# Low-plane scores by 64-row matmuls: both heads side by side, tiles two by two, one PSUM bank per head

## The chip, the core and the metric

The kernel runs on one core of one Trainium2 chip. The core has a matmul engine (TensorE, in the profile PE for matmuls and PEld for weight loads), VectorE (DVE), ScalarE (ACT), GpSimd (POOL) and SyncE (SP, which here only issues DMAs). Matmuls write to PSUM, which has eight banks of 2 KB per partition; everything else lives in SBUF, 128 partitions wide. The metric is the device time of one execution in microseconds, lower is better.

## The reference

Eight batches, eight heads of 64 dimensions, 512 local and 32 global positions. Local queries see all global keys and the local keys at most 32 positions away; global queries see everything. A feed-forward part with a cosine gate follows.

```python
s_g = scale * q_g @ concat(k_g, k_l).T ;  out_g = softmax(s_g) @ concat(v_g, v_l)
s_ll = where(|pos_q - pos_k| <= 32, scale * q_l @ k_l.T, -1e9)
out_l = softmax(concat(scale * q_l @ k_g.T, s_ll)) @ concat(v_g, v_l)
x = concat(out_g, out_l)  as (8*544, 512)
h = x @ w_in  (512 -> 2048);  out = (h * cos(h)) @ w_out  (2048 -> 512)
```

All inputs and the output are f32. The sums need more digits than one f16 matmul gives, so the kernel splits operands into a high and a low f16 plane.

## The kernel before

**Slots.** The whole work is written out by hand as events in numbered slots (`at(slot, phase, f, ...)`, line 1181). Inside a slot events are emitted in the order of their phase. A slot of the steady part holds one step of the feed-forward part (`m1_a` to `m1_d`, `m2_a`: 24 matmuls of 256 columns and 12 of 512, then elementwise work on ACT, DVE and POOL) and a few attention steps. Sixteen slots pass per batch, four per pair of heads. `steady` (line 1216) gives each step of a pair its slot. From the emitted order, a planner with a timeline of its own makes the final order of each engine: an instruction with no bank or operand ready in that timeline is passed by others. On the chip each engine's order is then fixed.

**Batches 0 and 1** take another path (`attn_pair_f`): scores straight from f32, 64 rows each, two heads in two banks (`f_qk`, line 607). It stays as it is.

**Batches 2 to 7**, one pair of heads at a time (24 pairs): `load_qk` brings queries (64 partitions) and keys (the other 64) of both heads; `qk_a` to `qk_c` find a scale, through a small matmul `pm_qk` (line 478) into PSUM; `qk_d` (lines 536, 537) writes the high plane to `qa` and the low plane to `kl`, each [128, 2 heads, 608]. `qk_e` (line 542) then moves partitions by DMAs from SP, in three steps that follow one another:

- step 0: high keys `qa[64:128]` to both halves of `kh` (lines 546, 547)
- step 1: low queries `kl[0:64]` to `qa[64:128]` (line 549)
- step 2: low keys `kl[64:128]` to `kl[0:64]` (line 551)

So `qa` holds high over low queries, `kh` the high keys twice and `kl` the low keys twice. `sc_a` (line 788) makes the scores of one tile of 128 queries against its window of 192 or 224 keys. Each head has two 128-row matmuls, with `kh` (line 794) and with `kl` (line 795), so that all four products of planes are summed. Both heads' scores go to one bank, `ps`. `sc_b` (line 810) reads them with VectorE, adds the mask and finds the row minimum `mn` (line 811); `sc_c` takes the exponential on ScalarE (line 440 is the helper `table_act`), `sc_d` normalises and splits, `sc_e` transposes by DMA, `av_a` multiplies with the values (`acc`, line 938). Pairs with an odd number also carry the global scores of two pairs, `g_a` (line 968), in two pieces: four heads in four column strips of 32, each with `kh` and then `kl` (line 977).

**Slots of the pieces before.** Counted from a pair's own slot t: copies at t-9 (steps 0 and 1) and t-8 (step 2), tiles 0 to 3 at t-7, t-6, t-5, t-4, each scored and read in its slot, the exponentials at t-4, global pieces at t-7 and t-6, the values at t. The next pair's `pm_qk` falls into slot t-7.

**PSUM.** Of the eight banks three have the tag "ph" (feed-forward in), two "po" (feed-forward out) and three "att". The scores `ps`, the global scores `gps`, `pm_qk` and `pm_v`, `acc` and `gacc` (the global output, line 1034) all take turns in the three of "att"; each is free again when its reader on VectorE (or ScalarE) is through.

Of the kernel before, what the change touches and what calls it, by code (L numbers as in the profile page):

```python
# [10 lines left out]
F32 = mybir.dt.float32  # L11
# [8 lines left out]
P = 128  # L20
# [3 lines left out]
SG = 32  # L24
# [12 lines left out]
WIN = ((0, 192), (128, 224), (256, 224), (416, 192))  # L37
OFF = (0, 0, 0, 32)
QZ = (32, 160, 320, 448)
WINF = ((0, 192), (128, 224), (256, 224), (384, 224))  # L40
MOFF = (0, 192, 416, 672)
MOFF_F = (0, 192, 416, 640)
# [48 lines left out]
s_load = -13  # L91
s_qa = -12
s_qd = -10
s_qe0 = -9
s_qe1 = -9
s_qe2 = -8
# [45 lines left out]
def body(tc, qk, qkf, v, wi, wo, mask, out):  # L142
    nc = tc.nc
# [4 lines left out]
    with ExitStack() as ctx:  # L148
        cp = ctx.enter_context(tc.tile_pool(name="cp", bufs=1))
        ap_ = ctx.enter_context(tc.tile_pool(name="ap", bufs=2))  # L150
        ps = ctx.enter_context(tc.tile_pool(name="ps", bufs=3, space=PSUM))
# [8 lines left out]
        msk = cp.tile([P, MW], BF16, name="msk")  # L160
# [3 lines left out]
        for i in range(4):  # L164
            t = cp.tile([P, 2, 2, 256], F16, name=f"planes{i}")
# [268 lines left out]
        st = {}  # L434
# [107 lines left out]
        def qk_e(b, p, k):  # L542
            qa, kh, kl, _ = st["qk", b, p]
            move = nc.vector.tensor_copy if b == 0 and SHV[p] else nc.sync.dma_start
            if k == 0:
                move(kh[0:64], qa[64:128])
                move(kh[64:128], qa[64:128])
            elif k == 1:
                move(qa[64:128], kl[0:64])
            else:  # L550
                move(kl[0:64], kl[64:128])

        def v_a(b):
            m = ap_.tile([P, 1], F32, tag="vm", name=f"vm_{b}")
# [52 lines left out]
        def f_qk(b, p, hf):  # L607
# [4 lines left out]
            for i in (2 * hf, 2 * hf + 1):  # L612
                z, w = WINF[i]
                for h in range(2):
                    r = slice(64 * h, 64 * h + 64)
                    nc.tensor.matmul(
                        pt[h][:, i % 2, :w], q[r, QZ[i] : QZ[i] + P], k[r, z : z + w],
                        start=True, stop=True,
# [3 lines left out]
        def f_tt(b, p, hf):  # L622
# [3 lines left out]
            for i in (2 * hf, 2 * hf + 1):  # L626
                w = WINF[i][1]
                t = ap_.tile([P, 2, w], F32, tag="t", name=f"t_{b}_{p}_{i}", bufs=6)
# [32 lines left out]
        def f_tr(b, p, hf):  # L661
# [4 lines left out]
            for k in range(2):  # L666
                tr = ps.tile([P, 4, P], F32, tag="att" if b else "ph", name=f"ftr_{b}_{p}_{hf}_{k}")
                n = 96 if k else P
                for i in range(2):
                    w = WINF[2 * hf + i][1] - P if k else P  # L670
                    for h in range(2):
# [12 lines left out]
        def f_av(b, p, hf):  # L684
# [9 lines left out]
            for n, (i, k, tl, q0, w) in enumerate((  # L694
                (i0, 0, i0, 0, 128), (i0 + 1, 0, i0 + 1, 0, 128 if hf == 0 else 96),
                (i0, 1, i0 + 1, 64 if hf == 0 else 32, 64 if hf == 0 else 96), (i0 + 1, 1, i0 + 2, 0, 128),
            )):
                kn = WINF[i][1] - P if k else P
                for h in range(2):
# [86 lines left out]
            )  # L786

        def sc_a(b, p, i):
            qa, kh, kl, al = st["qk", b, p]
            z, w = WIN[i]  # L790
            pt = ps.tile([P, 2, w], F32, tag="att", name=f"ps_{b}_{p}_{i}")
            for h in range(2):
                q = qa[:, h, QZ[i] : QZ[i] + P]
                nc.tensor.matmul(pt[:, h], q, kh[:, h, z : z + w], start=True, stop=False)
                nc.tensor.matmul(pt[:, h], q, kl[:, h, z : z + w], start=False, stop=True)
            st["ps", b, p, i] = pt

        def sc_b(b, p, i):
            w = WIN[i][1]
            al = st["qk", b, p][3]  # L800
            pt = st.pop(("ps", b, p, i))
            if b > 1 and i >= 2:
                if i == 2:
                    st["raw", b, p] = w2.tile([P, 512], I64, tag="raw", name=f"t_{b}_{p}_2")
                rf = st["raw", b, p].bitcast(F32)
                t = rf[:, (i - 2) * 512 : (i - 2) * 512 + 2 * w].rearrange("p (a b) -> p a b", a=2)
            else:
                t = ap_.tile([P, 2, w], F32, tag="t", name=f"t_{b}_{p}_{i}", bufs=6)
            mn = ap_.tile([P, 2], F32, tag="mn", name=f"mn_{b}_{p}_{i}", bufs=8)
            for h in range(2):  # L810
                nc.vector.tensor_tensor_reduce(  # L811
                    t[:, h], pt[:, h], msk[:, MOFF[i] : MOFF[i] + w], al, 3.0e38,
                    ALU.add, ALU.min, mn[:, h : h + 1],
                )
            if b < 2 and DEFN[b]:
                nc.vector.tensor_scalar(mn, mn, 14 * math.log(2.0), None, op0=ALU.add)
            st["t", b, p, i] = (t, mn)
# [150 lines left out]
        def g_a(b, g, k):  # L968
            z, w = GW[k]
            pt = ps.tile([P, w], F32, tag="att", name=f"gps_{b}_{g}_{k}")  # L970
            for hh in range(4):
                qa, kh, kl, _ = st["qk", b, 2 * g + hh // 2]
                h = hh % 2
                o = pt[32 * hh : 32 * hh + 32]
                q = qa[:, h, 0:SG]
                for kk in (kh, kl):
                    nc.tensor.matmul(
                        o, q, kk[:, h, z : z + w], start=(kk is kh), stop=(kk is kl),
                        tile_position=(0, 32 * hh), skip_group_check=True,
                    )  # L980
            st["gps", b, g] = pt

        def g_b(b, g, k):
# [197 lines left out]
        def at(slot, phase, f, *a):  # L1181
            ev[slot].append((phase, len(ev[slot]), f, a))

        def attn_pair(b, p, o):
            at(o["load"], PJ, load_qk, b, p)
            at(o["qa"], PF, qk_a, b, p)
            if o["tight"] or QB == 0:
                at(o["qa"], PG, qk_b, b, p)
                at(o["qa"], PG2, qk_c, b, p)
            else:  # L1190
                at(o["qa"] + 1, PA, qk_b, b, p)
                at(o["qa"] + 1, PB, qk_c, b, p)
            at(o["qd"], PF2, qk_d, b, p)
            for k in range(3):
                at(o["qe"][k], PA0 if k == 0 or o["tight"] else PJ, qk_e, b, p, k)
            for i in range(4):
                at(o["sc"][i], PA, sc_a, b, p, i)
                at(o["sc"][i], PA if o["tight"] else PC, sc_b, b, p, i)
                at(o["ex"], PI, sc_c, b, p, i)
                at(o["sd"], PF, sc_d, b, p, i)  # L1200
                at(o["tr"][i], PA2, sc_e, b, p, i)
            at(o["vd"], PF2, v_d, b, p)
            at(o["av"], PA, av_a, b, p)
            at(o["av"] if b else -6, PF, av_b, b, p)
            if p % 2:
                g = p // 2
                for k in range(2):
                    at(o["gs"][k], PA, g_a, b, g, k)
                    at(o["gs"][k], PA if o["tight"] else PC, g_b, b, g, k)
                at(o["ex"], PI, g_c, b, g)  # L1210
                at(o["gd"], PF2, g_d, b, g)
                at(o["ge"], PA2, g_e, b, g)
                at(o["gf"], PG, g_f, b, g)
                at(o["gf"], PH2, g_g, b, g)

        def steady(t, late=False):
            o = dict(
                load=t + s_load, qa=t + s_qa, qd=t + s_qd, qe=(t + s_qe0, t + s_qe1, t + s_qe2),
                sc=[t + s_sc0, t + s_sc1, t + s_sc2, t + s_sc3], ex=t + s_ex, sd=t + s_sd,
                tr=(t + s_tr,) * 4, vd=t + s_vd, av=t + s_av, gs=(t + s_gs0, t + s_gs1),  # L1220
                gd=t + s_gd, ge=t + s_ge, gf=t + s_gf, tight=False,
            )
            if late:
                o |= dict(load=t - 11, qa=t - 10, qd=t - 9, qe=(t - 8,) * 3)
            return o

        def tight(u, vd):
# [68 lines left out]
        for b in range(2, B):  # L1296
            t = 16 * (b - 1) + T0[b > 2]
            tv = max(t + s_v, 9)
            at(tv, PA0, load_v, b)
            at(tv + 1, PF, v_a, b)  # L1300
            at(tv + (1 if b == 2 else 2), PG if b == 2 else PA, v_b, b)
            at(tv + (1 if b == 2 else 2), PG2 if b == 2 else PB, v_c, b)
            for p in range(NPAIR):
                attn_pair(b, p, steady(t + 4 * p, b == 2 and p == 0))
# [52 lines left out]
def _mask():  # L1357
# [3 lines left out]
    cols = []  # L1361
    for i, (z, w) in enumerate(WINF):
        q = np.arange(i * P, (i + 1) * P)[:, None]
# [43 lines left out]
```

## Time and profile before

| | |
|---|---|
| median of 3 runs | 1025.35 us (1020.35 to 1028.5) |
| profiled execution | 1024.95 us, span 1022.9 us |
| granted TensorE clock, mean | 0.949 |
| PE busy | 917.1 us, 90% of the span |
| DVE, ACT, POOL busy | 644.6, 643.2, 621.7 us |
| 0 to 215 us, PE busy | 159.13 us (clock 0.79) |
| 215 to 845 us, PE busy | 589.36 of 630 us (clock 0.99) |
| 845 to 1022.9 us, PE busy | 168.57 of 177.9 us |

The first stretch is the start: weights, batches 0 and 1. The second holds the attention of batches 2 to 7 beside the feed-forward part. In the last one only the feed-forward part is left. A matmul's duration in the trace includes its way through the array, so that durations overlap; the distance from one start to the next tells what it costs. A line number such as L795 is that of the kernel before. A note in brackets at the end of a timeline row is the idle time before it and what ended it.

### The profile page before, as it was taken

How to read it: one execution, taken by the hardware profiler on the slowest of the kernel's cores; microseconds unless marked ns; L12 is line 12 of the kernel's file. 1: busy time of each engine (PE TensorE's matmuls, PEld its weight loads, DVE VectorE, ACT ScalarE, POOL GpSimd, SP SyncE). 2: the span in 40 equal slices, each digit the busy share in tenths (PEclk: the TensorE clock that was granted, in tenths of full speed). 3: DMA queues.
4: the chain of work that ended last, by engine and by line, in shares of the span. 5: the costliest groups of instructions: out<-in, count | busy, mean ns of one | idle time of the engine just before them, and what ended most of it. 6: DMA issues, size and time to landing. Idle time of an engine off the chain costs nothing.

```text
span 1022.9 us, 20754 instructions
## 1 busy us (share of the span) xinstructions
PE 917.1 (90%) x7847; PEld 626.1 (61%) x7847; DVE 644.6 (63%) x1575; ACT 643.2 (63%) x1298; POOL 621.7 (61%) x817
## 2 busy tenths in 40 slices
PE   7755788899888998998899899999999999999996
PEld 5534455566565666665676566666666666666662
DVE  5986867477767776767585758676866643332330
ACT  6543787657677576776677667767776775444330
POOL 4491564646675876775767476757676778444440
PEclk7756698999999999999999999999999999999999
DMA  9438013034545764453536454555454423000000
GB/s 376 170 122 347 1 42 108 1 122 125 122 90 120 137 141 104 103 120 117 122 84 130 127 124 93 124 142 124 92 118 98 100 43 76 1 22 1 22 21 21
DMA packets 141147, 106.11 MB, mean 104 GB/s; under 512 B 120440, under 2 KB 120440, under 8 KB 139000
## 3 DMA queue, kind: packets, MB, share of 16 engines
q1 hardware_dynamic: 141048, 104.80, 39.9%
q8 instruction: 61, 1.00, 0.4%
q14 instruction: 38, 0.31, 0.1%
HBM read 51.82 MB, written 8.91 MB: 59 GB/s over the span
## 4 chain that ended last, share of the span: by engine, by line
PE 30%; POOL 20%; DVE 19%; DMA 12%; ACT 11%; issue 6%; SPq 1%; POOLq 0%; ACTq 0%; DVEq 0%
PE ph L1096 13%; POOL t L873 6%; POOL planes L883 6%; DMA qkr<-qk 6%; PE po L1154 4%; PE po L1152 4%; PE po L1153 4%; ACT t L440 4%; DVE kl L537 3%; POOL w L1131 3%; DMA vr<-v 2%; DVE qm L496 2%; DVE u L1119 2%; ACT L440 2%; DVE gf L1133 2%
## 5 line engine op out<-in xcount | busy, mean ns | idle before, releaser
L1096 PE MATMUL ph<-xh,wi_h 128*128 128x256 f16 x1024 | 283.1, 277 | 17.4 <-DVE gf L1133 11.6
L1096 PE MATMUL ph<-xl,wi_h 128*128 128x256 f16 x1024 | 282.5, 276 | 0.9 <-DVE xl L718 0.9
L1096 PE MATMUL ph<-xh,wi_l 128*128 128x256 f16 x1024 | 282.3, 276 | 0.0
L1096 PEld LDWEIGHTS <-wi_h 128*128 128x128 f16 x2176 | 212.4, 99 | 69.3 <-issue 35.0
L1138 POOL TENSOR_TENSOR gl<-gf,gh 128x512 f16<-128x512 f32 x136 | 160.3, 1179 | 140.6 <-ACT gh L1137 140.6
L1152 PE MATMUL po<-wo_h,gh 128*128 128x512 f16 x544 | 206.9, 380 | 7.9 <-DVE o L1160 7.8
L1153 PE MATMUL po<-wo_l,gh 128*128 128x512 f16 x544 | 206.8, 380 | 0.0
L1154 PE MATMUL po<-wo_h,gl 128*128 128x512 f16 x544 | 206.6, 381 | 0.1
L1131 POOL TENSOR_TENSOR w<-w 128x512 f32<-128x512 f32 x136 | 145.6, 1071 | 77.8 <-ACT w L440 77.4
L1119 DVE SCALAR_TENSOR_TENSOR u<-u,cm,ph 128x512 f32<-128x512 f32 x136 | 101.2, 744 | 121.6 <-ACT u L1118 121.4
L1133 DVE SCALAR_TENSOR_TENSOR gf<-w,ph 128x512 f32<-128x512 f32 x136 | 93.1, 685 | 121.7 <-POOL w L1131 121.5
L1137 ACT CAST gh<-gf 128x512 f16<-128x512 f32 x136 | 83.3, 612 | 128.8 <-DVE gf L1133 127.4
L440 ACT ACTIVATE t<-t,mn 128x224 f32<-128x224 f32 (+1 forms) x256 | 117.3, 459 | 58.0 <-DVE mn L811 45.9
L873 POOL TENSOR_TENSOR t<-t,sm 128x192 f32<-128x192 f32 (+1 forms) x192 | 100.9, 557 | 78.2 <-DVE sm L858 76.1
L440 ACT ACTIVATE w<-u,ca 128x512 f32<-128x512 f32 x136 | 97.8, 721 | 74.8 <-DVE u L1119 71.5
L883 POOL TENSOR_TENSOR planes<-t,planes 128x192 f16<-128x192 f32 (+1 forms) x192 | 118.4, 646 | 0.0
L1096 PEld LDWEIGHTS <-wi_l 128*128 128x128 f16 x1088 | 107.4, 99 | 16.2 <-issue 2.2
L1118 ACT ACTIVATE u<-ph,cm 128x512 f32<-128x512 f32 x136 | 92.0, 677 | 14.1 <-PE ph L1096 14.0
L1154 PEld LDWEIGHTS <-gl 128*128 128x128 f16 x544 | 53.2, 98 | 62.9 <-issue 0.6
L1153 PEld LDWEIGHTS <-gh 128*128 128x128 f16 x544 | 53.2, 98 | 59.0 <-issue 10.7
L1152 PEld LDWEIGHTS <-gh 128*128 128x128 f16 x544 | 53.2, 98 | 49.3 <-issue 0.9
L440 ACT ACT_TABLE_LOAD x59 | 75.7, 1283 | 2.7 <-DVE gmn L744 1.7
(203 smaller groups left out, 1411.7 us busy)
## 6 DMA issues: line engine op xcount, KB each, us to landing
qkr<-qk SPq DMA_DIRECT2D x24, 608.0 KB, 4.7
vr<-v SPq DMA_DIRECT2D x8, 1280.0 KB, 8.6
out<-o SPq DMA_DIRECT2D x34, 256.0 KB, 2.0
kh<-qa SPq DMA_DIRECT2D x48, 152.0 KB, 2.6
wo_h<-wo SPq DMA_DIRECT2D x8, 512.0 KB, 4.4
wo_l<-wo SPq DMA_DIRECT2D x8, 512.0 KB, 4.8
raw_wo<-wo SPq DMA_DIRECT2D x8, 512.0 KB, 3.6
qa<-kl SPq DMA_DIRECT2D x24, 152.0 KB, 2.5
```

What stands on the lines that cost most here:

```text
L440: ins = nc.scalar.activation(*a, **k).ins
L873: nc.gpsimd.tensor_tensor(t[:, h], t[:, h], rb[:, h], op=ALU.mult)
L883: nc.gpsimd.tensor_tensor(lo[:, h], t[:, h], hi[:, h], op=ALU.subtract)
L1096: nc.tensor.matmul(ph[:, a], w[:, kc, f], x[:, kc, q], start=first and ip == 0, stop=last and ip == 2, skip_group_check=True,)
L1118: nc.scalar.activation(u, ph, AF.Identity, bias=m)
L1119: nc.vector.scalar_tensor_tensor(u, u, m, ph, op0=ALU.subtract, op1=ALU.subtract)
L1131: nc.gpsimd.tensor_tensor(w, w, w, op=ALU.mult)
L1133: nc.vector.scalar_tensor_tensor(gf, w, 0.5, st.pop(("ph", c, j)).rearrange("p a b -> p (a b)"), op0=ALU.subtract, op1=ALU.mult,)
L1138: nc.gpsimd.tensor_tensor(gl, gf, gh, op=ALU.subtract)
L1152: nc.tensor.matmul(po[k], gh[:, q], wo_h[:, f], start=(f == 0), stop=False)
L1153: nc.tensor.matmul(po[k], gh[:, q], wo_l[:, f], start=False, stop=False)
L1154: nc.tensor.matmul(po[k], gl[:, q], wo_h[:, f], start=False, stop=(f == NJ - 1))
```

## The change

For batches 2 to 7, the product of low queries with low keys is dropped, and the low keys meet the high queries alone, with 64 rows.

- The copies have four steps. Step 2 moves only head 0's low keys to the lower half. Step 3, new, moves head 1's high queries to the upper half of `kl`'s first slot, which step 2 has read. Head 0 then finds high queries and low keys on partitions 0 to 63, head 1 on 64 to 127. Steps 2 and 3 are both in slot t-8.
- `sc_a` works on tiles 0 and 1 at t-7 and on 2 and 3 at t-5, and does nothing at t-6 and t-4. It takes two banks, one for each head, and both tiles of a head share one (224 columns each). First come the four 128-row matmuls with `kh`, then four of 64 rows, the heads in turn. The reads by `sc_b` stay in their slots; each reads from both banks.
- `g_a` makes the four matmuls with `kh` first and then four 64-row ones.

```diff
-            else:
-                move(kl[0:64], kl[64:128])
+            elif k == 2:
+                move(kl[0:64, 0], kl[64:128, 0])
+            else:
+                move(kl[64:128, 0], qa[0:64, 1])
...
         def sc_a(b, p, i):
+            if i % 2:
+                return
             qa, kh, kl, al = st["qk", b, p]
-            z, w = WIN[i]
-            pt = ps.tile([P, 2, w], F32, tag="att", name=f"ps_{b}_{p}_{i}")
-            for h in range(2):
-                q = qa[:, h, QZ[i] : QZ[i] + P]
-                nc.tensor.matmul(pt[:, h], q, kh[:, h, z : z + w], start=True, stop=False)
-                nc.tensor.matmul(pt[:, h], q, kl[:, h, z : z + w], start=False, stop=True)
-            st["ps", b, p, i] = pt
+            pt = [
+                ps.tile([P, 2, FW], F32, tag="att", name=f"ps_{b}_{p}_{i // 2}_{h}") for h in range(2)
+            ]
+            for ii in range(i, i + 2):
+                z, w = WIN[ii]
+                for h in range(2):
+                    nc.tensor.matmul(
+                        pt[h][:, ii % 2, :w], qa[:, h, QZ[ii] : QZ[ii] + P], kh[:, h, z : z + w],
+                        start=(ii == i), stop=False, skip_group_check=True,
+                    )
+            for ii in range(i, i + 2):
+                z, w = WIN[ii]
+                for h in range(2):
+                    r = slice(64 * h, 64 * h + 64)
+                    nc.tensor.matmul(
+                        pt[h][:, ii % 2, :w], (kl if h else qa)[r, 0, QZ[ii] : QZ[ii] + P],
+                        kl[r, h, z : z + w], start=False, stop=(ii > i), skip_group_check=True,
+                    )
+                st["ps", b, p, ii] = [pt[h][:, ii % 2, :w] for h in range(2)]
...
-                for kk in (kh, kl):
-                    nc.tensor.matmul(
-                        o, q, kk[:, h, z : z + w], start=(kk is kh), stop=(kk is kl),
-                        tile_position=(0, 32 * hh), skip_group_check=True,
-                    )
+                nc.tensor.matmul(
+                    o, q, kh[:, h, z : z + w], start=True, stop=False,
+                    tile_position=(0, 32 * hh), skip_group_check=True,
+                )
+            for hh in range(4):
+                qa, kh, kl, _ = st["qk", b, 2 * g + hh // 2]
+                h = hh % 2
+                r = slice(64 * h, 64 * h + 64)
+                nc.tensor.matmul(
+                    pt[32 * hh : 32 * hh + 32], (kl if h else qa)[r, 0, 0:SG], kl[r, h, z : z + w],
+                    start=False, stop=True, skip_group_check=True,
+                )
...
-            for k in range(3):
+            for k in range(4):
                 at(o["qe"][k], PA0 if k == 0 or o["tight"] else PJ, qk_e, b, p, k)
```

More of the change, by code (lines that the diff above doesn't have):

```diff
@@ L39 @@
 QZ = (32, 160, 320, 448)
+FW = 224
 WINF = ((0, 192), (128, 224), (256, 224), (384, 224))
@@ L811, in sc_b @@
                 nc.vector.tensor_tensor_reduce(
-                    t[:, h], pt[:, h], msk[:, MOFF[i] : MOFF[i] + w], al, 3.0e38,
+                    t[:, h], pt[h], msk[:, MOFF[i] : MOFF[i] + w], al, 3.0e38,
                     ALU.add, ALU.min, mn[:, h : h + 1],
@@ L1217, in steady @@
             o = dict(
-                load=t + s_load, qa=t + s_qa, qd=t + s_qd, qe=(t + s_qe0, t + s_qe1, t + s_qe2),
+                load=t + s_load, qa=t + s_qa, qd=t + s_qd, qe=(t + s_qe0, t + s_qe1, t + s_qe2, t + s_qe2),
                 sc=[t + s_sc0, t + s_sc1, t + s_sc2, t + s_sc3], ex=t + s_ex, sd=t + s_sd,
@@ L1223, in steady @@
             if late:
-                o |= dict(load=t - 11, qa=t - 10, qd=t - 9, qe=(t - 8,) * 3)
+                o |= dict(load=t - 11, qa=t - 10, qd=t - 9, qe=(t - 8,) * 4)
             return o
```

## The prediction

> **What bounds the kernel now.** I read the page first, then the busy time by stretch, then the waits of the matmul engine, then the timelines of PE, DVE and SP in one stretch of the steady part.
>
> ```profile
> span 1022.9 us, 20754 instructions
> ...
> PE 917.1 (90%) x7847; PEld 626.1 (61%) x7847; DVE 644.6 (63%) x1575; ACT 643.2 (63%) x1298; POOL 621.7 (61%) x817
> ...
> PE   7755788899888998998899899999999999999996
> ...
> PEclk7756698999999999999999999999999999999999
> ```
>
> ```profile
> 215.00:845.00 630.00, 589.36 (x5484) 406.51 (x5482) 441.43 (x1062) 442.67 (x913) 431.30 (x572) 0.99 0.49 111
> ```
>
> The second fence is the stretch in which batches 2 to 7 go through the changed code (columns: length, then busy time of PE, PEld, DVE, ACT, POOL, then granted clock, DMA share, GB/s). PE is busy 589.36 of 630.00 us at a clock of 0.99; the next busiest engine has 442.67. So PE's order of work sets the end, and time goes in or out in two ways: array time per matmul, and holes in PE's stream. The holes of the whole run, by who ended them:
>
> ```profile
> PE ph L1096 <- DVE gf L1133: 11.6, 17, 1.8
> PE pm_qk L478 <- DVE mn L811: 10.0, 4, 2.8
> PE po L1152 <- DVE o L1160: 7.8, 7, 2.0
> PE ps L795 <- DMA kl<-kl: 3.5, 3, 2.4
> PE gacc L1034 <- DVE mn L811: 3.1, 4, 0.9
> ```
>
> (Total us, times, longest.) The second and the fifth are waits for a PSUM bank: pm_qk and gacc take a bank of the tag "att" and stand until VectorE has read a score tile (mn, line 811) out of it. The fourth is the wait for the key-plane copy that this change lengthens.
>
> **Array time of the scores.** One tile pair of the steady part, on PE:
>
> ```profile
> 501.00 0.25 PE L794 MATMUL ps<-kh,qa 128*128 128x192 f16 x1
> ...
> 501.25 0.25 PE L795 MATMUL ps<-kl,qa 128*128 128x192 f16 x1
> 501.43 0.32 PE L977 MATMUL gps<-kh,qa 128*32 128x288 f16 x4
> 501.56 0.31 PE L977 MATMUL gps<-kl,qa 128*32 128x288 f16 x4
> 501.80 0.23 PE L478 MATMUL pm_qk<-d_qk,ones 128*128 128x128 bf16 x1
> ...
> 507.07 0.26 PE L794 MATMUL ps<-kh,qa 128*128 128x224 f16 x1
> ...
> 507.36 0.26 PE L795 MATMUL ps<-kl,qa 128*128 128x224 f16 x1
> 507.55 0.30 PE L977 MATMUL gps<-kh,qa 128*32 128x256 f16 x4
> ```
>
> Durations overlap, so what counts is start to start. Four 192-column matmuls start at 501.00 to 501.25, so 0.083 us each; four of 224 from 507.07 to 507.36, so 0.097. A pair of heads has four low-plane tiles for two heads: 2 x (0.083 + 0.097 + 0.097 + 0.083) = 0.72 us. If the 64-row matmuls of the two heads run at once, 0.36 of that goes, in 24 pairs 8.6 us. Whether they do is shown by the 64-row f32 scores of batch 0, two stretches right behind one another:
>
> ```profile
> 19.59 1.76 PE L616 MATMUL fps<-kf,qf 64*128 64x192 f32 x8
> ```
>
> ```profile
> 21.14 1.70 PE L616 MATMUL fps<-kf,qf 64*128 64x224 f32 x4
> ```
>
> The four records of 21.14 are, as I read their even steps, one head alone: 1.70 less the last one's tail, 0.58, over three steps is 0.373 per 224 columns, 0.320 per 192. The eight of 19.59 are both heads, four of each width: one after the other they would take 2.77 us and the tail's rest of 0.2; they took 1.76. So two heads side by side do run in about half, in f32. For f16 I take the same.
>
> The number of matmuls and of weight loads stays (16 and 16 per pair). What is added is changes of the array's shape. The same rows price one: from 501.25 a 192-column matmul should be followed at 501.33, and the first 32-column tile starts at 501.43, so 0.10; from 507.36 + 0.097 to 507.55 it is 0.09. Back again: the four 288-column low matmuls start together at 501.56, 288 columns take 0.125 at this rate, and pm_qk starts at 501.80, 0.10 after that and the starts' 0.02. Into the 64-row shape, from full-array matmuls 0.109 apart:
>
> ```profile
> 133.79 0.27 PE L1096 MATMUL ph<-xl,wi_h 128*128 128x256 f16 x1
> 133.90 0.27 PE L1096 MATMUL ph<-xh,wi_l 128*128 128x256 f16 x1
> 134.10 1.02 PE L616 MATMUL fps<-kf,qf 64*128 64x224 f32 x4
> ```
>
> 134.10 less 133.90 is 0.20, so again 0.09. I take 0.10 for each, in and out. An even pair gets two low blocks, each between full-array work: four changes, 0.40 us against 0.36 saved. An odd pair has the global scores too. At the slot of its tile 0 the order was full, 32 columns, full (two changes) and becomes full, 64 rows, 32 columns, 64 rows by 32 columns, full (four); at tile 1's slot the scores are gone and the global block has one change more; tiles 2 and 3 add two: five, 0.50 us. So 12 x (0.40 + 0.50) = 10.8 us against 8.6: **+2.2 us**. The Trainium skill, page "TensorEngine Tiling (Array Packing)", section Theoretical Speedup, promises up to 2x when the contracted dimension is 64 or less; by that alone this term would be -8.6, and its list of key properties adds that a change of mode drains the array, which the 0.09 to 0.10 us here agree with.
>
> The global low plane stays as long as it was, since its four tiles ran side by side already, and 64-row by 32-column tiles do too: here the four first ones start within 0.02 us.
>
> ```profile
> 162.53 0.43 PE L731 MATMUL fgps<-qkr 64*32 64x288 f32 x2
> 162.54 0.43 PE L731 MATMUL fgps<-kf,qf 64*32 64x288 f32 x2
> 162.79 0.41 PE L731 MATMUL fgps<-qkr 64*32 64x288 f32 x2
> ```
>
> **The copies on SP.** The third move halves in bytes and a fourth follows that overwrites what the third reads, so SP waits for its landing. Pair 12:
>
> ```profile
> 517.71 0.46 SPq L549 DMA_DIRECT2D qa<-kl  x1
> 518.23 0.58 SPq L455 DMA_DIRECT2D qkr<-qk  x1
> 520.03 0.46 SPq L551 DMA_DIRECT2D kl<-kl  x1
> 534.56 0.46 SPq L546 DMA_DIRECT2D kh<-qa  x1
> ```
>
> ```profile
> 527.67 0.25 PE L794 MATMUL ps<-kh,qa 128*128 128x192 f16 x1
> ```
>
> ```profile
> DMA to landing us min/median/max: 2.3/3.2/7.8
> ```
>
> (The last is line 551's copy.) Move to move is 520.03 - 517.71 = 2.3 us. The fourth would go out near 522.4 and land near 525, against 527.67: hidden, with 2 to 3 us left of 5. Behind it on SP stand transposes, output stores and the next pair's first copy; here SP has nothing to issue until 534.56, and 24 issues of 0.46 us are 11 us of a queue that is mostly idle. Where the third copy is late (up to 7.8 us, and PE already waits three times, 3.5 us) the fourth adds its 2.3 to 3.2. Ends: 0, and 12.5 (five such pairs at 2.5, more than the three that are late now). I take the low side, **+2**, since the typical pair has room.
>
> **The PSUM banks.** Tag "att" has three. Two tiles by two heads are still four tiles in a pair, but they are taken two at once and each is held until both of its tiles are read. VectorE reads late:
>
> ```profile
> 505.50 0.41 DVE L811 CUSTOM_DVE_ANT_0 t<-ps,msk,al 128x192 f32<-128x192 f32 x1
> 505.83 0.08 DVE L811 DVE_READ_ACCUMULATOR2_ANT mn<- 128x1 f32 x1
> 505.83 0.41 DVE L811 CUSTOM_DVE_ANT_0 t<-ps,msk,al 128x192 f32<-128x192 f32 x1
> ...
> 506.17 0.51 DVE L994 CUSTOM_DVE_ANT_0 gt<-gps,zero,gal 128x288 f32<-128x288 f32 x1
> ...
> 506.61 0.28 DVE L510 TENSOR_REDUCE r<-pm_qk 128x2 f32<-128x128 f32 x1
> ```
>
> The tile written at 501.00 is read from 505.50 on. In an odd pair tile 0 (501.00), the global scores (501.43) and pm_qk (501.80) fill the three banks now. Afterwards the two score tiles and the global scores do, and pm_qk of the next pair waits until about 506.7. The planner will set it later in PE's order; what it misjudges becomes a hole. Rows for such a hole:
>
> ```profile
> 511.48 0.24 PE L1034 MATMUL gacc<-ptg,vh 128*64 128x32 f16 x4 [0.74 <-DVE mn L811]
> ```
>
> ```profile
> 581.95 0.27 PE L478 MATMUL pm_qk<-d_qk,ones 128*128 128x128 bf16 x1 [2.84 <-DVE mn L811]
> ```
>
> 0.74 is a matmul that the planner had placed where it thought the bank was free, which is the case here, so I take that: 12 odd pairs x 0.74 = 8.9 us, less the 3.1 of gacc, whose slot no longer has a score tile: **+5.8** (ends -3.1 and 12 x 2.84 = 34). The Trainium skill, same page, Gotcha 1: PSUM Pressure, says that row tiles write to different banks and so press on PSUM: it speaks against the change here, and no figure of it is used.
>
> **What comes earlier.** Tiles 1 and 3 are scored a slot before their turn, so VectorE can read them as soon as it is free, and ScalarE's exponentials wait for those reads now:
>
> ```profile
> L440 ACT ACTIVATE t<-t,mn 128x224 f32<-128x224 f32 (+1 forms) x256 | 117.3, 459 | 58.0 <-DVE mn L811 45.9
> ```
>
> An exponential that starts earlier lets ScalarE reach the next chunk's work earlier, and with it the reads that PE waits for (gf 11.6, o 7.8, together 19.4). Ends 0 and -19.4; ScalarE is idle for 45.9 us there but is no bound, so I take a fifth: **-4**.
>
> Sum on the profiled execution, 1024.95 us (span 1022.9 and 2.05 around it): +2.2 +2 +5.8 -4 = +6.0, 1031. The median of the runs, 1025.35, is 0.4 above it, which changes nothing: **1031 us**, 0.6% over.
>
> **Rivals.** *Banks bind* (slower): the hole at pm_qk is not 0.74 but 1.5 us, between the two rows, because VectorE reads the tile only after the next chunk's work; and the early reads give nothing back. 12 x 1.5 - 3.1 + 2.2 + 2 = +19, 1044. For: all three banks are full already, and pm_qk is the second largest wait. Against: the planner may push pm_qk past the hole. It decides above 0.77 us per odd pair (10.3 = 12 x 0.77 - 3.1 + 4.2).
>
> *Early scores pay* (faster): two thirds or more of the 19.4 come back and the banks cost nothing, so 2.2 + 2 - 13 to 2.2 + 2 - 19.4: -9 to -15, 1010 to 1016. For: ScalarE's 45.9 us of waiting. Against: those PE waits are 24, scattered, and one VectorE order is exchanged for another.
>
> *The changes of shape are hidden*: then -8.6 alone, 1016; with part of the early reads it passes 1%. That is the outcome by the tiling page's 2x. Against: every change of shape in the rows above costs 0.09 or more.
>
> *The last copy binds*: five late pairs, +12.5 + 2.2, 1040. Against: 2 to 3 us of room.
>
> *The heads do not run side by side in f16*: nothing is saved and 10.8 is paid, 1036. Against: the f32 rows.
>
> **How the numbers follow.** Chances: forecast 0.43 (own range 1024 to 1038, its four terms moved by half), banks 0.25, early scores 0.18, shapes hidden 0.05, last copy 0.05, not side by side 0.04. Runs of one kernel spread from 1020.35 to 1028.5, so 1% (10.3 us) is what can be told. Faster: two thirds of early scores and 0.03 of hidden shapes, 0.15. Slower: 0.22 of banks, 0.08 of the two small ones, 0.05 of the forecast's upper end, 0.35. Within 1%: the rest, 0.50. The range 1014 to 1044 leaves out the worse half of "banks" and the better half of "early scores", 2 in 10.
>
> **What would show it.** In the changed profile: two low matmuls of the two heads starting within 0.01 us of each other, and 0.08 to 0.10 for both; 0.09 to 0.10 us more at each change of shape, so PE's gain and loss about equal; in PE's waits, pm_qk for mn in odd pairs near 0.7 us each and gacc gone; ps for kl up by no more than 2 us; the holes before ph and po a little smaller. I am wrong if the low blocks show no such changes, if VectorE now reads tiles 0 and 1 back to back within 2 us of their scores (then the banks cost nothing), or if the planner's new order moves work far from the scores.

## The result, and the profile after

The changed kernel takes **1037.58 us** (median of 6 runs, 1033.25 to 1039.91) against 1025.09 (6 runs): a ratio of 1.012, 95% interval 1.0097 to 1.0144. It is slower by 12.5 us; the forecast was 6 us, in the same direction. The profiled execution took 1038.83 us.

From the page of the kernel after, its span and busy times:

```profile
span 1037.1 us, 20847 instructions
...
PE 935.0 (90%) x7847; PEld 624.8 (60%) x7847; DVE 623.9 (60%) x1575; ACT 645.2 (62%) x1298; POOL 617.7 (60%) x817
```

The number of matmuls is the same, and PE is busy 18 us longer. PE's waits over the whole run of the kernel after (total us, times, longest), to be held against the five rows of before:

```profile
PE pm_qk L479 <- DVE xl L980: 12.6, 6, 3.6
...
PE po L1176 <- ACT o L1186: 9.8, 6, 2.3
PE ph L1120 <- DVE gf L1157: 8.6, 8, 2.0
...
PE ps L809 <- DMA kl<-kl: 3.2, 3, 1.3
...
PE ps L809 <- DMA kl<-qa: 2.4, 2, 1.7
...
PE pm_qk L479 <- DVE mn L828: 1.4, 4, 0.3
...
PE gps L993 <- DVE xl L980: 0.9, 3, 0.4
```

The waits for score reads are almost gone: pm_qk for mn fell from 10.0 to 1.4 us, gacc for mn from 3.1 to nothing. In their place pm_qk waits 12.6 us for **xl**, VectorE's reading of the value accumulator `acc`, for which PE had no row before. All are waits for a bank of "att"; what changed is whose reader frees the first one.

Why xl is late is seen on ScalarE. First its group of exponentials in the kernel after (busy, mean ns, idle before them and its releasers):

```profile
L441 ACT ACTIVATE t<-t,mn 128x224 f32<-128x224 f32 (+1 forms) x256 | 117.0, 458 | 15.6 <-DVE mn L634 9.6 <-DVE mn L828 4.9 <-DVE ws L306 0.4
```

Before, 45.9 us of idle time stood there for mn; now it is 4.9. So the exponentials do find their data ready. Then the timeline of ScalarE around one pair of the kernel after (start, duration):

```profile
417.28 0.46 ACT L441 ACTIVATE t<-t,mn 128x192 f32<-128x192 f32 x1
...
420.47 0.44 ACT L441 ACTIVATE t<-t,mn 128x192 f32<-128x192 f32 x1
...
421.64 0.66 ACT L1142 ACTIVATE u<-ph,cm 128x512 f32<-128x512 f32 x1
...
423.24 1.28 ACT L441 ACT_TABLE_LOAD   x1
...
425.62 0.68 ACT L979 ACTIVATE xh<-acc,xs 128x512 f16<-128x512 f32 x1
```

All eight exponentials of the pair run in one go, then the global one, u, gh, planes, a table load, w and planes again (the dots leave some of them out), and only then **xh**, the first of the two reads of `acc`. ScalarE isn't idle for a moment: it does everything else first. VectorE waits for xh, and PE for VectorE, as their timelines in the same stretch show:

```profile
417.39 0.22 PE L955 MATMUL acc<-pt,vl 128*64 128x128 f16 x2
```

```profile
426.33 0.75 DVE L980 SCALAR_TENSOR_TENSOR xl<-acc,xs,xh 128x512 f16<-128x512 f32 x1 [2.18 <-ACT xh L979]
...
430.94 0.41 DVE L828 CUSTOM_DVE_ANT_0 t<-ps,msk,al 128x192 f32<-128x192 f32 x1
```

```profile
422.77 0.52 PE L801 MATMUL ps<-kh,qa 128*128 128x192 f16 x4
423.22 0.25 PE L809 MATMUL ps<-kl,qa 64*128 64x192 f16 x1
423.22 0.25 PE L809 MATMUL ps<-kl 64*128 64x192 f16 x1
423.31 0.26 PE L809 MATMUL ps<-kl,qa 64*128 64x224 f16 x1
423.32 0.26 PE L809 MATMUL ps<-kl 64*128 64x224 f16 x1
427.13 0.27 PE L479 MATMUL pm_qk<-d_qk,ones 128*128 128x128 bf16 x1 [3.56 <-DVE xl L980]
427.19 0.42 PE L1120 MATMUL ph<-xh,wi_h 128*128 128x256 f16 x1
427.40 0.42 PE L1120 MATMUL ph<-xl,wi_h 128*128 128x256 f16 x1
```

`acc` was complete at 417.6 and is read at 425.62 and 426.33. The new score tiles of 422.77 to 423.32 hold the other two banks, and VectorE, which has xl first in its order, reads them only from 430.94 on. So all three banks are taken, the first to come free is that of `acc`, and pm_qk, next in PE's order, stands 3.56 us. It is the same in all six waits of pm_qk for xl: the score tiles are read 2.7 to 3.8 us after pm_qk has started. Before, xh came between the exponentials of tiles 2 and 3 (the ScalarE timeline of the kernel before):

```profile
548.77 0.67 ACT L962 ACTIVATE xh<-acc,xs 128x512 f16<-128x512 f32 x1
551.77 0.46 ACT L440 ACTIVATE t<-t,mn 128x192 f32<-128x192 f32 x1 [2.33 <-DVE mn L811]
```

Tile 3's exponential had to wait for its scores there, and xh went ahead of it. Over all 24 pairs the median time from the last acc matmul to xh is 2.58 us before and 5.72 after (worked out from the starts of those rows).

One thing more follows a hole. PE's matmuls from 427.19 on start 0.21 us apart instead of 0.11: the granted clock is halved there (0.50), for a stretch of 3.41 us.

To see where the time lies I split the middle part, from ScalarE's u of feed-forward step 8 to that of step 112, by PE's distances from start to start. A hole is what a distance has beyond the matmul's columns (0.42 ns each, from the 0.215 us between two starts of po's matmuls with 512) where PE was idle for more than 0.06 us; the column "half clock" is what full-array matmuls took longer in stretches at half clock; the last one is the length less those two. Changes of shape are counted where PE had no such idle time (with the others they are 120 before and 246 after).

| kernel | length, us | holes | half clock | changes of shape | rest |
|---|---|---|---|---|---|
| before | 684.8 | 49.1 | 3.1 | 116 | 632.5 |
| after | 698.8 | 52.6 | 9.7 | 225 | 636.5 |
| full rows | 697.1 | 55.7 | 7.4 | 115 | 634.1 |
| by turns | 693.6 | 37.9 | 8.3 | 332 | 647.4 |
| xh first | 673.7 | 35.7 | 1.7 | 222 | 636.4 |
| full rows, xh first | 675.7 | 38.7 | 3.3 | 119 | 633.8 |
| by turns, xh first | 674.5 | 27.7 | 0.0 | 330 | 646.9 |
| before, xh first | 681.0 | 45.4 | 3.4 | 116 | 632.2 |

From before to after: +14.0 us, of which holes +3.5, half clock +6.5, array +4.0. That tells where the length lies in one execution of each, not what each part would give back. The first and the last row are two executions of the same sequence of instructions on every engine, so their distance, 3.8 us in length and 3.7 in holes, shows the spread of such a row. The rows below the second are the experiments.

### The profile page after: what moved, and what is told of

Same layout as the page of the kernel before. It is cut to its first block, busy times and chain, and to the rows that moved or that the text cites. A ratio compares the mean times of both kernels' runs of the same rounds, so it can differ in the third digit from the quotient of the medians.

```text
span 1037.1 us, 20847 instructions
## 1 busy us (share of the span) xinstructions
PE 935.0 (90%) x7847; PEld 624.8 (60%) x7847; DVE 623.9 (60%) x1575; ACT 645.2 (62%) x1298; POOL 617.7 (60%) x817
## 4 chain that ended last, share of the span: by engine, by line
PE 26%; POOL 22%; ACT 16%; DVE 15%; DMA 13%; issue 7%; SPq 1%; POOLq 0%; ACTq 0%; DVEq 0%
PE ph L1120 11%; POOL planes L900 8%; ACT t L441 6%; POOL t L890 5%; DMA qkr<-qk 5%; POOL w L1155 4%; PE po L1176 4%; PE po L1177 4%; PE po L1178 4%; ACT L441 2%; POOL gl L1162 2%; DMA vr<-v 2%; DVE kl L538 2%; DVE u L1143 2%; ACT u L1142 1%
## 5 line engine op out<-in xcount | busy, mean ns | idle before, releaser
L1162 POOL TENSOR_TENSOR gl<-gf,gh 128x512 f16<-128x512 f32 x136 | 164.1, 1208 | 117.3 <-ACT gh L1161 117.3
L1155 POOL TENSOR_TENSOR w<-w 128x512 f32<-128x512 f32 x136 | 141.7, 1043 | 115.9 <-ACT w L441 113.2
L900 POOL TENSOR_TENSOR planes<-t,planes 128x192 f16<-128x192 f32 (+1 forms) x192 | 115.2, 633 | 0.0
```

Of the source, the lines that this page charges most:

```text
L900: nc.gpsimd.tensor_tensor(lo[:, h], t[:, h], hi[:, h], op=ALU.subtract)
L1155: nc.gpsimd.tensor_tensor(w, w, w, op=ALU.mult)
L1162: nc.gpsimd.tensor_tensor(gl, gf, gh, op=ALU.subtract)
```

## The experiments

Two theories. **Array**: the 109 further changes of shape cost more than side by side saves. **Order**: the scores that come two tiles early let ScalarE run all exponentials before xh; `acc` keeps its bank, and the holes and the half clock behind them are the loss. The short edits are against the kernel after, where nothing else is said; lines of the longer kernels shift by a few.

### Full rows in the new order

```diff
-            else:
-                move(kl[64:128, 0], qa[0:64, 1])
...
-                        pt[h][:, ii % 2, :w], (kl if h else qa)[r, 0, QZ[ii] : QZ[ii] + P],
-                        kl[r, h, z : z + w], start=False, stop=(ii > i), skip_group_check=True,
+                        pt[h][:, ii % 2, :w], qa[:, h, QZ[ii] : QZ[ii] + P],
+                        kl[:, h, z : z + w], start=False, stop=(ii > i), skip_group_check=True,
```

Step 2 moves both heads again, and the global scores are as before.

> The changed kernel with its banks and its order of tiles (two tiles by two, one bank per head), but the low plane by 128-row matmuls as before, with the three copies and the global scores of before: no change of shape is added and nothing runs side by side. Theory 'shapes' (the loss is the 109 added changes of shape less the saved columns, about 4 us in the trace): 1033 if the rest of the loss is the banks. Theory 'banks' (two banks held at once, pm_qk standing after the scores, and the half-clock windows that follow): stays at 1030 to 1036, with pm_qk waiting 8 us or more in sum and more than two half-clock windows between 215 and 845 us. If neither the banks nor the order cost anything: 1025, as before.

Measured: 1035.84 us, 1.0114 (1.0085 to 1.0142). Nearly the whole loss is there without one 64-row matmul in batches 2 to 7. Its waits of PE:

```profile
PE po L1167 <- ACT o L1177: 17.0, 7, 3.3
...
PE pm_qk L479 <- DVE xl L978: 11.1, 8, 2.7
```

So the array theory falls as the main cause; what is left for it, 1.7 us, is inside the spread.

### High and low plane by turns

```diff
-            for ii in range(i, i + 2):
                 z, w = WIN[ii]
                 for h in range(2):
                     r = slice(64 * h, 64 * h + 64)
```

Each tile's low plane follows its high plane, so that a pair has two changes of shape more for each two tiles.

> The changed kernel, but high and low by turns, tile by tile, so that each tile pair has four changes of shape and not two: 96 changes more in 24 pairs, the same columns, banks and copies. Theory 'shapes' at 0.095 us each: +9 us over the changed kernel, 1047. If changes of shape cost nothing on the path: 1038, no difference.

Measured: 1036.71 us, 1.012 (1.0076 to 1.0165). The table counts 107 changes more, and the rest rose by 10.9 us, 0.10 each, but the holes fell by 14.7 and the time didn't rise. Array time at this place is taken in by the holes.

### Without the fourth copy

```diff
-            else:
-                move(kl[64:128, 0], qa[0:64, 1])
```

Head 1's low plane then meets other data, so a part of its scores is left out; the matmuls are the same in number and shape.

> The changed kernel without the fourth copy: head 1's low plane then meets what lies in that buffer, so that part of the scores is left out, and all matmuls stay. Theory 'fourth copy binds': back by 4 us or more, to 1033 or less. Otherwise (PE stood 2.4 us for that copy): 1035 to 1038.

Measured: 1035.44 us, 1.0104 (1.0078 to 1.0131), 2.1 us less than the kernel after. That is the size of the wait for kl<-qa (2.4), but within the spread of the runs; pm_qk for xl stays (11.8 us).

### Both tiles read in the slot of their scores

```diff
-                at(o["sc"][i], PA if o["tight"] else PC, sc_b, b, p, i)
+                at(o["sc"][i - i % 2], PA if o["tight"] else PC, sc_b, b, p, i)
```

> The changed kernel with VectorE's reads of tiles 1 and 3 put into the slot of their scores, a slot earlier, so that both banks come free earlier. Theory 'banks': the holes at pm_qk shrink if it is the score banks that are waited for: 1030. If it is the value accumulator's bank that pm_qk waits for (the trace has xl as the releaser), nothing is gained: 1036 to 1039. Theory 'shapes' alone: no difference, 1037.

Measured: 1030.34 us, 1.006 (1.0039 to 1.008). Waits of PE:

```profile
PE po L1176 <- ACT o L1186: 18.2, 8, 2.8
...
PE pm_qk L479 <- DVE xl L980: 5.1, 5, 1.4
```

PE waits 7.5 us less for the bank of `acc`, but 8.4 us more in another wait for ScalarE: po, the feed-forward output, waits for `o`, which stands behind the same block of exponentials. These two rows cancel, and yet the run is 7.2 us shorter than the kernel after: the time is the one expected if the score banks are what is waited for, while the waits that are left name `acc`. So early reads of the scores are worth something here, and how was not isolated. In the kernel after one such hole before po is this, first ScalarE, then PE:

```profile
557.15 0.44 ACT L441 ACTIVATE t<-t,mn 128x192 f32<-128x192 f32 x1
...
558.67 0.68 ACT L1186 ACTIVATE o<-po,co 128x512 f32<-128x512 f32 x1
```

```profile
559.40 0.38 PE L1176 MATMUL po<-wo_h,gh 128*128 128x512 f16 x1 [2.25 <-ACT o L1186]
```

### xh ahead of tile 3's exponentials

```diff
+                if i in (3,) and 4 * b + p - 1 in xh_ins:
+                    tc.add_manual_dep(
+                        last_act["Exp"], xh_ins[4 * b + p - 1].name, order, reason="xh_first"
+                    )
...
-            nc.scalar.activation(xh[:, p], acc, AF.Identity, scale=sx)
+            xh_ins[4 * b + p] = nc.scalar.activation(xh[:, p], acc, AF.Identity, scale=sx).ins
```

The planner is only told an order of two instructions on ScalarE; nothing else is written differently, but it plans all engines anew from that.

> The changed kernel, but ScalarE's exponentials of tile 3 stand behind its evacuation of the value accumulator (xh) of the pair before, as they do in the kernel before; nothing else is edited. Theory 'ScalarE's order' (the early scores let the exponentials pass xh, so that the accumulator's bank comes free late and pm_qk stands on PE): the wait of pm_qk for xl (12.6 us) falls below 3 us, and the time to 1026 to 1031. Theory 'banks' (the score tiles themselves hold too many banks): no gain, 1035 to 1038, or pm_qk waits for mn in its place.

Measured: **1016.35 us, 0.9913 (0.988 to 0.9946)**: 21 us off the kernel after, and faster than before. The wait fell as expected, the time 10 us further than either theory gave. Waits of PE:

```profile
PE po L1182 <- DVE o L1190: 9.3, 8, 2.0
PE ph L1126 <- DVE gf L1163: 8.5, 11, 1.8
...
PE pm_qk L481 <- DVE xl L986: 1.7, 3, 0.6
...
PE pm_qk L481 <- DVE mn L830: 1.2, 4, 0.3
```

pm_qk's waits are down from 14.0 to 2.9 us, and po waits for VectorE's o and no longer for ScalarE's. The place that was shown above, on ScalarE, VectorE and PE:

```profile
415.43 0.68 ACT L985 ACTIVATE xh<-acc,xs 128x512 f16<-128x512 f32 x1
416.01 0.45 ACT L443 ACTIVATE t<-t,mn 128x192 f32<-128x192 f32 x1
```

```profile
416.76 0.74 DVE L986 SCALAR_TENSOR_TENSOR xl<-acc,xs,xh 128x512 f16<-128x512 f32 x1
```

```profile
417.86 0.26 PE L811 MATMUL ps<-kl 64*128 64x224 f16 x1
418.05 0.23 PE L481 MATMUL pm_qk<-d_qk,ones 128*128 128x128 bf16 x1
```

xl is over at 417.50 and pm_qk follows the scores at once. The median from acc to xh is 2.59 us, as before. In the table holes fall by 16.9 us and the half clock by 8.0: together the whole difference of 25.1 in length. The order theory stands, for ScalarE's order as a whole. On the chip the edit does more than put xh in front: held against each other by name and shape, 184 of ScalarE's 1298 instructions stand in another order in the kernel after than before, and 47 in this run, in which u and gh are ahead of tile 3's exponentials again too; 166 of VectorE's 1575 moved with them. How much of the 21 us is xh's alone isn't shown.

### Tiles 2 and 3 a slot later

```diff
-s_sc2 = -5
+s_sc2 = -4
```

> The changed kernel with tiles 2 and 3 scored together in tile 3's slot (t-4), behind the accumulator's matmuls, and not in tile 2's (t-5). Theory 'ScalarE's order': xh comes ahead of their exponentials again, pm_qk's wait for xl falls, 1026 to 1032. Theory 'banks': two banks are still taken at once, 1035 to 1038.

Measured: 1052.6 us, 1.0275 (1.0239 to 1.0311): 20 us slower than expected, and more than either theory gave. The group of exponentials again shows 45.9 us of idle time for mn, and xh comes 1.63 us behind acc (median), so the early start is undone as meant, but the waits of PE show what late scores cost:

```profile
PE ph L1120 <- DVE gf L1157: 16.9, 11, 2.2
PE acc L955 <- DMA pt<-planes: 12.7, 11, 4.4
...
PE ps L801 <- DVE mn L828: 9.6, 16, 1.9
PE pm_qk L479 <- DVE mn L828: 9.4, 8, 1.3
```

The value matmuls now wait for the transposes, and scores and pm_qk for banks. With two tiles to a block, this slot is too late for it.

### pm_qk in a bank of "ph"

```diff
-            early = name.startswith(("qk0", "v0"))
+            early = name.startswith(("qk", "v0"))
```

> The changed kernel with pm_qk of batches 2 to 7 in one of the feed-forward banks (tag ph) and not in att; xh stays as late as it is. Theory 'ScalarE's order' and theory 'banks' both let the wait at pm_qk go, 12.6 us: 1026 to 1031 if those holes are the loss, unless ph itself runs short (then PE's ph waits for gf, 8.6 us now, rise by what pm_qk gave). If the holes only move to the waits of po for o (9.8 now): 1034 to 1038.

Measured: 1031.18 us, 1.0064 (1.0041 to 1.0088). The wait of pm_qk for xl is gone, and a part of it comes back in the banks that it borrows. Waits of PE:

```profile
PE ph L1120 <- DVE gf L1157: 16.7, 15, 2.3
...
PE po L1176 <- ACT gh L1161: 6.8, 3, 2.4
```

The holes of the middle part are 45.3 us, 7.3 less than after: the bank is a part of the loss. The waits of po for gh (6.8 us, a row that neither before nor after has) suggest that ScalarE's order reaches PE by other ways too; that wasn't isolated.

### The kernel before with a late xh

```diff
-            nc.scalar.activation(xh[:, p], acc, AF.Identity, scale=sx)
+            ins = nc.scalar.activation(xh[:, p], acc, AF.Identity, scale=sx).ins
+            tc.add_manual_dep(ins, last_act["Exp"].name, order, reason="xh_late")
...
-            at(o["av"] if b else -6, PF, av_b, b, p)
+            at(o["av"] if b else -6, PJ, av_b, b, p)
```

The last line moves `av_b`, that is xh and xl, to the end of its slot, behind the exponentials that it is to follow.

> The kernel before, with xh put behind the last exponential of its slot and nothing else. Theory 'ScalarE's order': about half of the changed kernel's loss or more, 1030 to 1037, with waits of pm_qk or of scores for xl that the kernel before does not have. Theory 'banks': one bank per tile leaves room for it, 1024 to 1028.

Measured: 1027.47 us, 1.0021 (1.0 to 1.0042), less than the order theory gave and inside the range of the other, though xh is later than in the kernel after (median 6.46 us behind acc against 5.72). Waits of PE:

```profile
PE pm_qk L478 <- DVE mn L811: 5.9, 4, 2.7
...
PE pm_qk L478 <- DVE xl L964: 4.0, 6, 0.9
```

pm_qk waits 9.9 us, as it did (10.0). With scores that take one bank at a time a late xh costs about 2 us, at the edge of the spread. So a late xh alone isn't the loss either; beside two banks that go to scores at once pm_qk waits 12.6 us for xl, here 4.0.

### Is the array the bound once the holes are gone?

The same two-line order on top of "full rows" and of "by turns":

> The order edit of the earlier run (xh of the pair before goes ahead of the exponentials of tile 3) on top of the kernel whose low plane is made by 128-row matmuls in the same two banks. It has some 110 changes of shape fewer than that run, and 0.36 us more array time a pair. Theory A, with the holes gone the array's time is the bound again: the side by side form costs what its changes of shape cost less what it saves, by the trace of the kernel after against that with full rows 636.5 - 634.1 = 2.4 us, so this run ends 2 to 3 us before 1016.35, near 1014. Theory B, the holes still take such differences in: within 1 us of 1016.35, or above it.

> The same order edit with high and low plane by turns, tile by tile: some 107 changes of shape more, 0.10 us each, 10.9 us of array time by the earlier traces. Theory A, the array binds: 1026 to 1028. Theory B, the holes take it in, as they did without the order edit (1036.71 against 1037.58): 1015 to 1019, and the holes in the middle part fall from 35.7 us to below 28.

Measured: 1016.08 us, 0.9926 (0.9902 to 0.9951), and 1014.42 us, 0.9921 (0.9894 to 0.9949). By the table their array time lies 13.1 us apart (633.8 and 646.9) and the number of changes is 119 and 330, yet the times agree with each other and with 1016.35. I had expected 10 us between them: theory A fell, theory B held. For full rows alone the two theories lie within the spread; "by turns" decides. It is a clean pair with "xh first": ScalarE, GpSimd and SyncE have the same sequence of instructions in both. PE is 91 to 92% busy, but what it does more of at this place comes out of its waits, as the row of "by turns, xh first" shows (holes 27.7 against 35.7 and 38.7).

### Early reads and the order together

> The same order edit, and both tiles of a bank pair are read in the slot of their scores. If what is left of the wait for banks (pm_qk for mn 1.9 us and for xl 2.2 us, acc 0.9) goes and nothing comes in its place: 1012 to 1015. If VectorE's earlier reads put off its work for the feed-forward part, as in the run with early reads alone (wait of po for o 18.2 us against 9.8): 1018 to 1028.

Measured: 1013.92 us (1013.15 to 1016.34), 0.991 (0.9888 to 0.9931), within the spread of the other three. pm_qk waits 2.1 us in all instead of 2.9; po for o is 8.0 us, so VectorE's earlier reads no longer hurt.

### The kernel before with the order alone

> The kernel before with the order edit alone. Theory A, the edit only mends what the early scores broke, since before xh stood ahead of tile 3's exponentials already (548.77 against 551.77): 1023 to 1027, waits of PE as before (gf 11.6, mn 10.0, o 7.8). Rival: the edit is worth as much by itself: 1005 to 1015.

Measured: 1023.33 us against 1023.13, 1.0 (0.9983 to 1.0017). Waits of PE:

```profile
PE pm_qk L480 <- DVE mn L813: 9.0, 4, 2.9
```

xh stood there already, and the sequence of instructions is the same as before on every engine: the run repeats the kernel before. So the edit changes something only where the early scores have moved xh, and the gain of the run with xh first needs the early scores.

## Why the prediction was right or wrong

**The time** was inside the range and the sign of the forecast right, but the change was twice the forecast, +12.5 us against +6.0, and the way there was partly wrong.

**Array time, +2.2.** The mechanism and the size were right in the trace. The low matmuls of the two heads start within 0.01 us (423.22 and 423.22); 108 changes of shape were counted in advance, 126 came, 109 of them where PE didn't stand anyway; with full rows the rest is 634.1 against 636.5, so 2.4 us. Against the kernel before the rest rose by 4.0; the other 1.6 is in the full rows too and isn't the shape's. The 2x of the Trainium skill (page "TensorEngine Tiling (Array Packing)", section Theoretical Speedup) is there in the starts, two matmuls at 423.22 and two from 423.31 on, but not in the time: side by side or not makes 1037.58 or 1035.84, and 1016.35 or 1016.08 with xh first. What was wrong is the first step, that PE's order sets the end and that array time and holes can be added. "By turns" added 10.9 us of array time once and 10.5 once more, and the time stayed both times.

**The fourth copy, +2.** Waits of ps for kl went from 3.5 to 5.6 us (3.2 and 2.4), and the run without it was 2.1 us shorter: right as far as these runs can tell.

**The banks, +5.8.** That the bank of pm_qk is the place of the loss was right, and so was that two score tiles are held until VectorE reads them late. Wrong was the third bank and the pairs: I had it taken by the global scores, in odd pairs, and freed by mn, 0.74 us each. Waits for mn fell by 11.7 us (10.0 + 3.1 to 1.4); it is `acc` that holds the third bank and frees it first, mainly in even pairs, for 12.6 us at pm_qk and 0.9 at gps.

**What comes earlier, -4.** This is the step that failed, a gain where a loss came. Its first half was right: ScalarE's 45.9 us of waiting went to 4.9. From that I concluded that ScalarE would reach the next work sooner. On an engine with a fixed order, data that is ready early moves the *order*: the planner put eight exponentials, and more behind them, ahead of xh and o, which PE needs first. The waits that I wanted to shorten stayed (gf and o: 19.4 before, 18.4 after), and a new one came, the 12.6 us of pm_qk for xl. With ScalarE's order put back the same kernel takes 1016.35 us. The last of the things that I named as making me wrong, work moved by the planner's new order, was the one that happened; I gave it no price.

**Not in the sum: the clock.** Six stretches of 3.4 us at half clock in the middle part instead of two, +6.5 us of the table's 14.0. I had taken the 0.99 of that part as given. How much of it is loss isn't shown: the traces without the fourth copy and with early reads have eight such windows each, and these executions were 4 and 5 us shorter than that of the kernel after.

**The rivals.** "Banks bind" had the right place, and score tiles that are read late, but not the reader that frees the third bank; its price, 1044, was 6 us too high. "Early scores pay" (1010 to 1016) lost on the kernel as it was written. The same kernel with one order added takes 1016.35, but that is its number and not its mechanism: the waits for gf and o, from which it wanted 13 us or more, are 17.8 there against 19.4. What went are the waits for mn, 13.1 to 1.2. The full-row version reaches the same, so it is the early tiles, two by two, and not the 64-row form, that pay there.

**Open.** Which chain of engines paces the middle part when holes take in 10 us of array time wasn't isolated: with "by turns" the waits for o, gf, the copies and the banks all shrink a little. Early scoring without the second bank wasn't tried, nor xh moved with every other instruction left in place.

## What to carry to other kernels

When a change makes data ready earlier, ask which instructions on the reader's engine will now be placed in front of which others, and whether one of those pushed back frees a buffer that the busiest engine needs. Apart, a late release cost about 2 us, and a second held buffer showed no cost (that run is faster than before); the changed kernel, which has both, lost 12.5 us. A busy share of 90% does not make an engine's work additive: test it by adding work of a known size at the place, as "by turns" did, before saving work there. And price the half clock behind a long hole: after the 3.56 us at pm_qk PE's matmuls took 1.5 us more (14 distances of 0.21 instead of 0.11).

## What the hardware showed that was not expected

**Half clock follows idle time within one window of 3.41 us, and the windows don't move.** All half-clock stretches of a trace begin on one grid of 3.413 us (in the kernel after at 328.00, 426.99, 481.60, 560.11, 669.33, 778.56: multiples of 3.4133 apart, 29, 16, 23, 32 and 32), wherever the holes are. The kernel after, the window with the hole of 2.25 us before po and the next one (length, busy time of PE, PEld, DVE, ACT, POOL, then the clock):

```profile
556.69:560.10 3.41, 1.16 (x9) 0.60 (x7) 1.78 (x4) 3.39 (x10) 1.83 (x4) 1.00 0.01 2
560.11:563.52 3.41, 3.41 (x10) 1.22 (x9) 0.75 (x1) 3.40 (x7) 3.41 (x7) 0.50 0.42 156
```

PE is idle for 2.25 of 3.41 us in the first, and the second is at half clock. With xh first there was a longer hole, 3.70 us up to 311.99, but a border of the grid cut it in two, and the clock stayed:

```profile
306.59:310.00 3.41, 1.70 (x16) 1.27 (x14) 2.87 (x3) 1.38 (x3) 3.22 (x2) 1.00 0.90 223
310.00:313.41 3.41, 1.42 (x12) 1.13 (x13) 3.24 (x9) 3.38 (x11) 1.04 (x1) 1.00 0.86 177
313.42:316.83 3.41, 3.41 (x22) 1.78 (x21) 1.18 (x3) 2.56 (x8) 2.31 (x2) 1.00 0.11 26
```

Idle times are 1.71 and 1.99 us. I counted the windows between 215 and 850 us of all 14 traces of this case by the idle time of PE in them: of 40 with 2.1 us or more, all 40 were followed by a window at half clock; of 29 between 1.77 and 2.1, 12; of 2535 with less, 7. So 2.1 us of idle time within a window were always followed by half clock here, while the hole of 3.70 us wasn't. The Trainium skill, page "TensorE: Matmul & The Clock Gate", section "What's actually happening", states a freely running window of 3413 ns, with which the grid agrees; its rule of no idle gaps over about 3 us (section "Why this matters for your kernels") doesn't fit these counts: a hole of 2.25 us halved the clock and one of 3.70 us didn't.

**A change of shape cost the same wherever it stood.** 0.10 us a change by the two "by turns" kernels (10.9 / 107 and, against "xh first", 10.5 / 108), the value that the rows of before gave.
